# Loading q and k on 128 partitions instead of 96 in a fused attention and two-layer feed-forward kernel

## The chip, the cores and the metric

The kernel runs on one core of a Trainium2 chip. A core has a matmul engine (TensorE, in the profile PE, with PEld for its weight loads), a vector engine (DVE), a scalar engine (ACT), a general engine (POOL) and a queue engine (SP) that here issues nearly all transfers; sixteen DMA engines carry them. Each engine works through its own list of instructions in order and waits on semaphores for the others. The metric is device microseconds (us) of one execution, lower is better.

## The reference, cut to what matters

```python
def sm_attn(qq, kk, vv):                       # scale = 1/8
    s = scale * qq @ kk.T ; s = s - max(s) ; a = exp(s)
    return (a / (sum(a) + 1e-9)) @ vv
p_packed = sm_attn(p, k, v)                    # 32 packed rows read 576 tokens
out      = sm_attn(q, p_packed, p_packed)      # 576 tokens read the 32 rows
x = out as (4*576, 8*64)
g = softplus(x @ w_in) ; x = g @ w_out         # 512 -> 2048 -> 512
out = (sigmoid(x @ w_gate) * (x @ w_val)) @ w_out2   # 512 -> 1536 -> 512
```

q, k and v are (4 batches, 8 heads, 576 tokens, 64), in 32-bit floats; p has 32 rows in place of 576. The weights come in 64-bit floats and are made 32-bit on the chip.

## The kernel before, in words

Attention is cut into eight units u0 to u7: a batch and half of its heads (four). Each unit needs one load of k, q and v (576 KB each, four heads) and a small one of p. `load_kqv` (L216) issues the loads in the order of a plan as soon as the memory region given for it is free: k0, k1, q0, v0, q1, v1, then k2, q2, v2, k3 and so on. A load puts 96 partitions to use: partition r takes six neighbouring tokens (6r to 6r+5) of each of the four heads, so a contiguous piece is 6 x 64 numbers, 1536 bytes.

`attn_unit` (L367) is a generator of stages with a `yield` between them:

- k to its transposed form kT: `by_chunk` (L335) lets POOL copy one pair of heads from the loaded tile into x, [96, 6, 2, 64]; `tr_pair` (L344) then lets TensorE transpose six blocks of 96 tokens x 128 columns into two PSUM banks, from which ACT copies 288 columns each (L356). Twice, for two pairs of heads. kT's tokens then lie as c*96 + r for token 6r + c.
- s1 (L387): p against kT; the first softmax on DVE and ACT (L395 to L407, in place in a1, normalised at L407).
- q the same way as k into qT (L409 to L414).
- a1 transposed in six blocks of 96 tokens (L421), copied by ACT to a1T (L422).
- the product with v (L440), twelve filler matmuls for the first three units (L365), the result copied by ACT into bdT (L94).
- s2 (L465): q against the packed rows; the second softmax on DVE, ACT and POOL (L475 to L483), transposed (L493) and split in two parts as operand A2h, A2l of the feed-forward layers.

Since a1's tokens lie in the same order as v's (both six to a partition), L421 takes neighbouring columns. The token order of q goes through the whole feed-forward part, and the final store undoes it with a view of the output (L992, L1016).

Units 0 to 3 run ahead; then the first layer (L111 to L113 inside `emit_h`, after the first weights are folded with the packed rows at L570) starts, and units 4 to 7 are slipped between its matmuls. Beside that, weights are loaded into a ring of two raw tiles and converted on DVE by three instructions each (L178, L183, L187); each conversion done lets SP issue the next weight load (L153, L155). The tile framework orders each engine's list by its own planning, so a change of shapes can also change the order of instructions. A DMA that takes one of eight completion semaphores waits until the DMA eight places earlier on it has landed.

Of the kernel before, what the change touches and what calls it, by code (L numbers as in the profile page):

```python
# [9 lines left out]
F32 = mybir.dt.float32  # L10
F32R = mybir.dt.float32r
I32 = mybir.dt.int32
AF = mybir.ActivationFunctionType
ALU = mybir.AluOpType
# [6 lines left out]
def attn_moe_moe_kernel(  # L21
# [21 lines left out]
    nc = tc.nc  # L43
    B, H, S, D = q.shape
# [4 lines left out]
    P = 128  # L49
    NC = 6  # L50
    CT = S // NC
    HS = S // 2
    CF = 256
    NCH1 = F1 // CF
    NCH2 = F2 // CF
# [12 lines left out]
    VCH = 8  # L68
    VSP = 0
# [14 lines left out]
    xa = cst.tile([P, KD * NT], F32, name="xa")  # L84
# [4 lines left out]
    def bank1():  # L89
        return ps_o[-1].tile([P, 512], F32, tag="o", name="ps1")  # L90
# [26 lines left out]
    att = tc.alloc_tile_pool(name="att", bufs=1, side="right")  # L117
# [14 lines left out]
    for c in range(NCH1):  # L132
        order += [("in", c, f) for f in range(2)] + [("out", c, f) for f in range(2)]
        if c > ECS:
            n = -(-len(early) // (NCH1 - c))
# [78 lines left out]
    KQV = 4 * NC * D  # L214

    def load_kqv():  # L216
        while plan and plan[0][2] not in busy:
            nm, u, tag = plan.popleft()
            b, g = divmod(u, 2)
            if tag == 6:  # L220
                t = att.tile([CT, KQV], F32, tag="acc6", name=f"{nm}{u}")
            else:
                t = xa[:CT, KQV * tag : KQV * (tag + 1)]
            src = {"k": k, "q": q, "v": v}[nm][b, 4 * g : 4 * g + 4]
            if nm == "v" and u >= VCH:
                t = t.rearrange("p (c h d) -> p c h d", c=NC, h=4)
                for hh in range(4):
                    nc.sync.dma_start(t[:, :, hh], src[hh].rearrange("(r c) d -> r c d", c=NC)) if VSP else None
                if not VSP:
                    nc.sync.dma_start(t, src.rearrange("h (r c) d -> r c h d", c=NC))  # L230
            else:
                t = t.rearrange("p (h c d) -> p h c d", h=4, c=NC)
                nc.sync.dma_start(t, src.rearrange("h (r c) d -> r h c d", c=NC))
            if nm == "k" and u + 1 < 2 * B:
                load_p(u + 1)
            kqv[nm, u] = t
            busy[tag] = (nm, u)
# [24 lines left out]
    ident = cst.tile([P, P], F32, name="ident")  # L262
# [56 lines left out]
    MULA = 0  # L319
# [6 lines left out]
    E1 = nc.scalar  # L326
# [5 lines left out]
            :, :, :NK  # L332
        ]

    def by_chunk(src, j):  # L335

        x = att.tile([CT, NC, 2, D], F32, tag="x", bufs=2, name="x")
        nc.gpsimd.tensor_scalar(
            x, src[:, 2 * j : 2 * j + 2].rearrange("p h c d -> p c h d"), 1.0, 0.0,
            op0=ALU.mult, op1=ALU.add,  # L340
        )
        return x

    def tr_pair(src, j, dst, eng):  # L344
        x = by_chunk(src, j)
        for hf in range(2):
            ps = bank1()
            for c in range(3):
                nc.tensor.transpose(
                    ps[:, c * CT : (c + 1) * CT],  # L350
                    x[:, 3 * hf + c].rearrange("p h d -> p (h d)"),
                    ident[:CT, :CT],
                )
            o = dst[:, j, hf * HS : (hf + 1) * HS]
            if eng is nc.scalar:
                eng.activation(o, ps[:, :HS], AF.Copy)  # L356
            else:
                eng.tensor_copy(o, ps[:, :HS])

    def warm(u, to, n):  # L360

# [5 lines left out]
    def attn_unit(u):  # L367
        b, g = divmod(u, 2)
# [3 lines left out]
        for e in range(2):  # L372
            r = slice(64 * e, 64 * e + 64)
# [2 lines left out]
            )  # L376
        kt = kqv.pop(("k", u))
        kT = att.tile([P, 2, S], F32, tag="kT", bufs=1, name="kT")
        tr_pair(kt, 0, kT, nc.scalar)
        yield  # L380
        tr_pair(kt, 1, kT, E1)
        done_kqv("k", u)
        yield
        s1 = bank2()
# [16 lines left out]
        )  # L401
        nc.vector.tensor_scalar(mx[:, 2:3], mx[:, 2:3], 1e-9, None, op0=ALU.add)
        nc.vector.reciprocal(mx[:, 3:4], mx[:, 2:3])
        if MULA:
            nc.scalar.activation(a1, a1, AF.Copy, scale=mx[:, 3:4])
        else:
            nc.vector.tensor_scalar(a1, a1, mx[:, 3:4], None, op0=ALU.mult)  # L407
        yield
        qt = kqv.pop(("q", u))  # L409
        qT = att.tile([P, 2, S], F32, tag="qT", bufs=2, name="qT")  # L410
        tr_pair(qt, 0, qT, nc.scalar)
        yield
        tr_pair(qt, 1, qT, E1)
        done_kqv("q", u)  # L414
        yield
        a1T = att.tile([CT, NC, P], F32, tag="a1T", bufs=2, name="a1T")
        for hf in range(2):
            pa = bank1()
            for c in range(3):
                o = (3 * hf + c) * CT  # L420
                nc.tensor.transpose(pa[:CT, c * P : (c + 1) * P], a1[:, o : o + CT], ident)  # L421
            nc.scalar.activation(  # L422
                a1T[:, 3 * hf : 3 * hf + 3].rearrange("p c n -> p (c n)"),
                pa[:CT, : 3 * P], AF.Copy,
            )
# [563 lines left out]
        add(v1, u, v1)  # L989
        result(s1, v1, 0)  # L990

    outv = out.rearrange("(b r c) m -> b c r m", r=CT, c=NC)  # L992
    NTT = HB * S // P

    def emit_out2(ps, c, t):
# [15 lines left out]
        if c == NCH2 - 1:  # L1011
            t0 = ps * HB * S + t * P
            a, e = t0, t0 + P
            while a < e:
                b, r = divmod(a, S)
                cc, r = divmod(r, CT)  # L1016
                n = min(e - a, CT - r)
                eng = nc.scalar if ps and a > t0 else nc.sync
                eng.dma_start(outv[b, cc, r : r + n, :], acc[a - t0 : a - t0 + n])
                a += n  # L1020
# [65 lines left out]
```

## Time and profile before

| | us |
|---|---|
| median of three timed runs (866.4 to 867.51) | 866.66 |
| span of the profiled execution, first to last instruction | 864.4 |
| what lies around the span, taken as the difference | 2.3 |
| TensorE busy in the span | 840.7 |
| granted TensorE clock | 1.000 |

The profile has one execution; its own time is listed only as its span, so the difference of 2.3 us to the median stands for what lies around it. TensorE is busy for 97% of the span, which says that little time is left in waits, and where the rest of 24 us lies: in the first 60 us most of all, before and while the attention units run ahead. A busy TensorE isn't at its peak, since matmuls overlap in its pipeline and their ends are modelled.

### The profile page before, as it was taken

Reading aid. Unit: us, or ns where it says so; the run is one execution under the profiler, and the core shown is the slowest. Engines: PE = TensorE matmul, PEld = TensorE weight load, DVE = VectorE, ACT = ScalarE, POOL = GpSimd, SP = SyncE. Lnnn points to the kernel's source line nnn. Section 1 sums busy time; section 2 is a strip of 40 time slices with the busy share of each in tenths; the row PEclk is TensorE's granted clock in tenths of the full one; section 3 lists DMA queues with packets and bytes.
Section 4 is the critical chain, followed back from the end, with each engine's and each line's share of the span. In section 5 each row is a group of like instructions: output and inputs, shape, how many; then the busy total and the mean of one; then the engine's idle time right before and its main releaser. Section 6 shows DMA issues by size and latency. Waiting matters only on the chain. (4 is left out here: it accounts for less than half of the span.)

```text
span 864.4 us, 15635 instructions
## 1 busy us (share of the span) xinstructions
PE 840.7 (97%) x6100; PEld 789.8 (91%) x6100; DVE 618.2 (72%) x1051; ACT 401.1 (46%) x721; POOL 474.7 (55%) x453
## 2 busy tenths in 40 slices
PE   6899999999999999999899999999999999999997
PEld 5788999899999999999898999999988999999995
DVE  2875556957576767668898788887896756767665
ACT  4567565576666656677533432222352432322210
POOL 4454333235555545685569787876984734536400
PEclk9999999999999999999999999999999999999999
DMA  9984330303023412300055555644515313213003
GB/s 237 225 212 91 82 82 3 92 7 99 2 96 101 127 27 82 119 26 1 1 165 187 161 164 148 201 129 131 162 53 156 112 47 86 67 43 111 14 1 109
DMA packets 58009, 85.55 MB, mean 99 GB/s; under 512 B 6352, under 2 KB 39248, under 8 KB 57936
## 3 DMA queue, kind: packets, MB, share of 16 engines
q1 hardware_dynamic: 56928, 83.31, 34.3%
q10 hardware_dynamic: 1008, 1.25, 0.4%
q8 instruction: 48, 0.79, 0.4%
q14 instruction: 25, 0.20, 0.1%
HBM read 65.67 MB, written 18.87 MB: 98 GB/s over the span
## 5 line engine op out<-in xcount | busy, mean ns | idle before, releaser
L111 PE MATMUL bank<-aop,BH 128*128 128x288 f32 x672 | 199.2, 296 | 3.1 <-DVE work L954 1.4
L113 PE MATMUL bank<-aop,BL 128*128 128x288 f32 x672 | 198.8, 296 | 0.6 <-POOL BL L99 0.6
L112 PE MATMUL bank<-aop,BH 128*128 128x288 f32 x672 | 197.8, 294 | 0.2 <-DVE aop L99 0.2
L99 POOL TENSOR_TENSOR ghl<-g,ghl 128x576 fp32r<-128x576 f32 x64 | 93.7, 1465 | 133.0 <-ACT ghl L106 132.8
L653 PE MATMUL ps<-ghl,woh 128*128 128x288 f32 x512 | 148.7, 305 | 3.0 <-DVE xa L661 2.6
L661 DVE TENSOR_TENSOR xa<-xa,ps 128x288 f32<-128x288 f32 x224 | 98.4, 449 | 70.4 <-PE ps L656 70.1
L654 PE MATMUL ps<-ghl,wol 128*128 128x288 f32 x512 | 143.3, 295 | 0.0
L111 PEld LDWEIGHTS bank<-aop,BH 128*128 128x128 f32 x672 | 126.2, 188 | 9.3 <-issue 1.5
L112 PEld LDWEIGHTS bank<-aop,BH 128*128 128x128 f32 x672 | 126.4, 188 | 4.1 <-DVE aop L99 0.4
L113 PEld LDWEIGHTS bank<-aop,BL 128*128 128x128 f32 x672 | 126.5, 188 | 0.9 <-POOL BL L99 0.9
L99 POOL TENSOR_TENSOR BL<-cv,BH 128x512 fp32r<-128x512 f32 (+1 forms) x96 | 117.9, 1243 | 4.9 <-ACT BH L106 3.8
L656 PE MATMUL ps<-ghl,woh 128*128 128x288 f32 x512 | 109.0, 294 | 0.1
L653 PEld LDWEIGHTS ps<-ghl,woh 128*128 128x128 f32 x512 | 96.2, 188 | 6.0 <-issue 2.4
L654 PEld LDWEIGHTS ps<-ghl,wol 128*128 128x128 f32 x512 | 96.3, 188 | 0.5
L954 DVE TENSOR_TENSOR work<-work,bank 128x576 f32<-128x576 f32 (+1 forms) x100 | 70.8, 724 | 29.2 <-PE bank L113 29.0
L1002 PE MATMUL ps<-ol,gv 128*128 128x512 f32 x216 | 84.9, 393 | 0.0
L1001 PE MATMUL ps<-oh,gv 128*128 128x512 f32 x216 | 84.4, 391 | 0.5 <-ACT gv L967 0.4
L1003 PE MATMUL ps<-oh,gv 128*128 128x512 f32 x216 | 84.8, 393 | 0.0
L983 ACT ACTIVATE work<-bank 128x576 f32<-128x576 f32 (+1 forms) x25 | 15.8, 634 | 143.8 <-DVE bank L954 143.8
L656 PEld LDWEIGHTS ps<-ghl,woh 128*128 128x128 f32 x512 | 82.1, 188 | 0.3 <-POOL ghl L99 0.3
L1009 DVE TENSOR_TENSOR xa<-xa,ps 128x512 f32<-128x512 f32 x90 | 61.5, 684 | 28.3 <-PE ps L1003 27.8
L111 PE MATMUL ps<-A2h,wph 128*128 128x288 f32 x256 | 77.6, 303 | 0.1
(126 smaller groups left out, 1747.9 us busy)
## 6 DMA issues: line engine op xcount, KB each, us to landing
cv<-B SPq DMA_DIRECT2D x52, 256.0 KB, 2.7
B<-cv SPq DMA_DIRECT2D x48, 256.0 KB, 4.2
raw_in<-in_moe_w_in_dram SPq DMA_DIRECT2D x16, 512.0 KB, 3.7
raw_out<-in_moe_w_out_dram SPq DMA_DIRECT2D x16, 512.0 KB, 3.6
raw_g<-in_moe_w_gate_dram SPq DMA_DIRECT2D x12, 512.0 KB, 4.4
raw_v<-in_moe_w_val_dram SPq DMA_DIRECT2D x12, 512.0 KB, 4.6
raw_o<-in_moe_w_out_dram SPq DMA_DIRECT2D x12, 512.0 KB, 4.2
xa<-in_q_dram SPq DMA_DIRECT2D x6, 576.0 KB, 7.0
```

The source lines that it names most:

```text
L99: eng.tensor_tensor(lo, x, hi.bitcast(F32), op=ALU.subtract)
L111: nc.tensor.matmul(ps, wh, xh, start=first, stop=False)
L112: nc.tensor.matmul(ps, wh, xl, start=False, stop=False)
L113: nc.tensor.matmul(ps, wl, xh, start=False, stop=last)
L653: nc.tensor.matmul(out_, wh[:, ms], gh[:, f], start=f == 0, stop=False)
L654: nc.tensor.matmul(out_, wl[:, ms], gh[:, f], start=False, stop=False)
L656: nc.tensor.matmul(out_, wo_hl[c, f][0][:, ms], gl[:, f], start=False, stop=f == 1)
L661: nc.vector.tensor_tensor(dst, dst, out_, op=ALU.add)
L954: nc.vector.tensor_tensor(to, x, y, op=ALU.add)
L1001: nc.tensor.matmul(bank, gh[:, ts_], oh, start=f == 0, stop=False)
L1002: nc.tensor.matmul(bank, gh[:, ts_], ol, start=False, stop=False)
L1003: nc.tensor.matmul(bank, gl[:, ts_], oh, start=False, stop=f == 1)
```

## The change

q and k are loaded on all 128 partitions: for each pair e of two heads, 64 partitions with nine neighbouring tokens each (a contiguous piece of 9 x 64 numbers, 2304 bytes). That takes two DMAs per load in place of one, e = 0 into partitions 0 to 63 and e = 1 into 64 to 127. v stays as it was, on 96 partitions. `turn` replaces `by_chunk` and `tr_pair`: three times per load POOL copies three token places of both pairs, [128, 3, 2, 64], TensorE transposes three blocks of 128 x 128 into one bank, and ACT copies 384 columns. The tokens of k, and so of a1, now lie as c*64 + r for token 9r + c, those of v still six to a partition; the normalisation of the first softmax therefore writes a new tile a1n in token order (a step of nine numbers), and the transposes of a1n read it with a step of six numbers. The output view follows q's order.

```diff
+    NQ = 9
+    RQ = S // NQ
...
-            if nm == "v" and u >= VCH:
...
-            else:
-                t = t.rearrange("p (h c d) -> p h c d", h=4, c=NC)
-                nc.sync.dma_start(t, src.rearrange("h (r c) d -> r h c d", c=NC))
+            else:
+                t = t[:, : 2 * NQ * D].rearrange("p (i x) -> p i x", i=2)
+                for e in range(2):
+                    nc.sync.dma_start(
+                        t[RQ * e : RQ * e + RQ],
+                        src[2 * e : 2 * e + 2].rearrange("i (r c) d -> r i (c d)", c=NQ),
+                    )
+                t = t.rearrange("p i (c d) -> p c i d", c=NQ)
...
+    def turn(src, n, dst):
+        x = att.tile([P, 3, 2, D], F32, tag="x", bufs=3, name="x")
+        nc.gpsimd.tensor_scalar(x, src[:, 3 * n : 3 * n + 3], 1.0, 0.0, op0=ALU.mult, op1=ALU.add)
+        ps = bank1()[:, : 3 * P]
+        for c in range(3):
+            nc.tensor.transpose(
+                ps[:, c * P : (c + 1) * P], x[:, c].rearrange("p i d -> p (i d)"), ident
+            )
+        nc.scalar.activation(
+            dst[:, :, 3 * RQ * n : 3 * RQ * (n + 1)].rearrange("p e (c r) -> p e c r", r=RQ),
+            ps.rearrange("p (c e r) -> p e c r", e=2, r=RQ), AF.Copy,
+        )
...
-        tr_pair(kt, 0, kT, nc.scalar)
-        yield
-        tr_pair(kt, 1, kT, E1)
+        for n in range(3):
+            turn(kt, n, kT)
+            if n == 1:
+                yield
...
-            nc.vector.tensor_scalar(a1, a1, mx[:, 3:4], None, op0=ALU.mult)
+        a1n = att.tile([P, S], F32, tag="a1n", bufs=1, name="a1n")
+        nc.vector.tensor_scalar(
+            a1n.rearrange("p (r c) -> p c r", c=NQ), a1.rearrange("p (c r) -> p c r", c=NQ),
+            mx[:, 3:4], None, op0=ALU.mult,
+        )
...
-                nc.tensor.transpose(pa[:CT, c * P : (c + 1) * P], a1[:, o : o + CT], ident)
+                nc.tensor.transpose(
+                    pa[:CT, c * P : (c + 1) * P],
+                    a1n.rearrange("p (r c) -> p c r", c=NC)[:, 3 * hf + c], ident,
+                )
...
-    outv = out.rearrange("(b r c) m -> b c r m", r=CT, c=NC)
+    outv = out.rearrange("(b r c) m -> b c r m", r=RQ, c=NQ)
```

The change moves instructions too. On ACT, around the copies of unit 1's packed rows into bdT (line L94 before, L96 after), with the exponentials of unit 0's second softmax (L479), the list before reads:

```order
L94 ACTIVATE bdT<-ps_279 64x2x32 x2
L422 ACTIVATE a1T<-ps_319 96x384
L422 ACTIVATE a1T<-ps_324 96x384
L479 ACTIVATE a_337<-a_337 96x384
L94 ACTIVATE bdT<-ps_361 64x2x32
L479 ACTIVATE a_353<-a_353 96x384
L94 ACTIVATE bdT<-ps_361 64x2x32
```

and after:

```order
L96 ACTIVATE bdT<-ps_275 64x2x32 x2
L422 ACTIVATE a1T<-ps_316 96x384
L422 ACTIVATE a1T<-ps_321 96x384
L479 ACTIVATE a_334<-a_334 96x384
L479 ACTIVATE a_350<-a_350 96x384
L96 ACTIVATE bdT<-ps_358 64x2x32 x2
```

The second exponential has moved from between the two copies of unit 1 to ahead of both.

On DVE, where the first two w_in tiles are converted (L178, L183, L187 before; L180, L185, L189 after) beside unit 1's first softmax (mx, a_225 or a1n) and unit 0's second (m, a), the list before reads:

```order
L178 TENSOR_SCALAR w_in<-raw_in 128x4x128
L402 TENSOR_SCALAR mx<-mx 128x1
L183 SCALAR_TENSOR_TENSOR w_in<-raw_in,w_in 128x4x128
L403 RECIPROCAL mx<-mx 128x1
L187 SCALAR_TENSOR_TENSOR w_in<-raw_in,w_in 128x4x128
L407 TENSOR_SCALAR a_225<-a_225,mx 128x576
L178 TENSOR_SCALAR w_in<-raw_in 128x4x128
L183 SCALAR_TENSOR_TENSOR w_in<-raw_in,w_in 128x4x128
L187 SCALAR_TENSOR_TENSOR w_in<-raw_in,w_in 128x4x128
L475 TENSOR_REDUCE m_336<-ps_329 96x12
L476 TENSOR_TENSOR a_337<-ps_329,m_336 96x384
```

and after:

```order
L401 TENSOR_SCALAR a1n<-a_227,mx 128x9x64
L180 TENSOR_SCALAR w_in<-raw_in 128x4x128
L185 SCALAR_TENSOR_TENSOR w_in<-raw_in,w_in 128x4x128
L189 SCALAR_TENSOR_TENSOR w_in<-raw_in,w_in 128x4x128
L180 TENSOR_SCALAR w_in<-raw_in 128x4x128
L185 SCALAR_TENSOR_TENSOR w_in<-raw_in,w_in 128x4x128
L475 TENSOR_REDUCE m_333<-ps_326 96x12
L475 TENSOR_REDUCE m_349<-ps_342 96x12
L476 TENSOR_TENSOR a_334<-ps_326,m_333 96x384
L476 TENSOR_TENSOR a_350<-ps_342,m_349 96x384
L189 SCALAR_TENSOR_TENSOR w_in<-raw_in,w_in 128x4x128
```

Unit 1's first softmax now stands ahead of the conversions, and the last conversion of the second tile behind four instructions of unit 0's second softmax.

On SP, from the third k load on (raw_out is a load of w_out, k_305 and k_301 are k3), before:

```order
L233 DMA xa<-in_k_dram 96x4x384
L153 DMA raw_out<-in_moe_w_out_dram 128x1024
L282 DMA p<-in_p_dram 128x64
L153 DMA raw_out<-in_moe_w_out_dram 128x1024
L282 DMA p<-in_p_dram 128x64
L233 DMA xa<-in_q_dram 96x4x384
L233 DMA xa<-in_v_dram 96x4x384
L233 DMA k_305<-in_k_dram 96x4x384
```

and after:

```order
L233 DMA xa<-in_k_dram 64x2x576 x2
L155 DMA raw_out<-in_moe_w_out_dram 128x1024
L286 DMA p<-in_p_dram 128x64 x2
L155 DMA raw_out<-in_moe_w_out_dram 128x1024
L233 DMA xa<-in_q_dram 64x2x576 x2
L229 DMA xa<-in_v_dram 96x4x384
L233 DMA k_301<-in_k_dram 64x2x576 x2
```

The loads keep their order; each load of q and k has become two rows, and q2, v2 and k3 still stand behind the second w_out load.

## Rows read from the trace of the kernel before

**Rows 1.** The page: busy time of the engines, and TensorE in forty slices of 21.6 us.

```profile
PE 840.7 (97%) x6100; PEld 789.8 (91%) x6100; DVE 618.2 (72%) x1051; ACT 401.1 (46%) x721; POOL 474.7 (55%) x453
PE   6899999999999999999899999999999999999997
```

**Rows 2.** Windows: stretch, length, busy time of PE, PEld, DVE, ACT, POOL, clock, DMA share, GB/s.

```profile
3.00:18.00 15.00, 10.84 (x63) 9.02 (x64) 2.66 (x7) 6.10 (x20) 6.84 (x9) 1.00 1.11 252
18.00:21.00 3.00, 2.61 (x59) 2.38 (x57) 1.28 (x5) 2.43 (x8) 0.00 (x0) 1.00 1.11 343
21.00:40.00 19.00, 16.71 (x181) 14.00 (x178) 15.09 (x39) 8.85 (x26) 8.06 (x10) 1.00 0.99 236
40.00:60.00 20.00, 18.64 (x194) 16.03 (x193) 16.43 (x33) 13.97 (x35) 10.29 (x9) 1.00 0.83 200
60.00:160.00 100.00, 99.33 (x962) 91.55 (x963) 62.31 (x148) 61.47 (x138) 38.14 (x38) 1.00 0.28 67
```

**Rows 3.** Timeline of POOL: start, duration, instruction, count, idle time before and releaser.

```profile
5.97 1.63 POOL L338 TENSOR_SCALAR x<-xa 96x768 f32<-96x768 f32 x2 [2.67 <-DMA xa<-in_k_dram]
11.72 0.83 POOL L338 TENSOR_SCALAR x<-xa 96x768 f32<-96x768 f32 x1 [1.04 <-DMA xa<-in_q_dram]
...
16.27 1.63 POOL L338 TENSOR_SCALAR x<-xa 96x768 f32<-96x768 f32 x2 [1.78 <-PE ps L387]
```

**Rows 4.** Timeline of TensorE from 16 to 40 us.

```profile
16.08 0.66 PE L349 MATMUL ps<-ident,x 96*128 96x96 f32 x6
17.15 0.71 PE L349 MATMUL ps<-ident,x 96*128 96x96 f32 x6 [0.41 <-POOL x L338]
17.70 0.82 PE L421 MATMUL ps<-ident,a 128*96 128x128 f32 x6
...
19.89 1.24 PE L440 MATMUL ps<-a1T,xa 96*64 96x32 f32 x36 [0.39 <-ACT a1T L422]
...
23.26 2.25 PE L465 MATMUL ps<-bdT,qT 128*96 128x64 f32 x24
...
29.53 2.25 PE L465 MATMUL ps<-bdT,qT 128*96 128x64 f32 x24 [0.96 <-ACT bdT L94]
...
36.84 0.47 PE L493 MATMUL ps<-ident,a 96*128 96x96 f32 x3 [0.66 <-POOL a L483]
37.63 0.47 PE L493 MATMUL ps<-ident,a 96*128 96x96 f32 x3 [0.32 <-POOL a L483]
...
39.81 0.40 PE L111 MATMUL ps<-A2h,wph 128*128 128x288 f32 x1
```

**Rows 5.** Timeline of ACT around 29 us.

```profile
28.61 0.22 ACT L94 ACTIVATE bdT<-ps 64x64 f32<-64x64 f32 x1 [2.38 <-PE ps L365]
28.73 0.51 ACT L479 ACTIVATE a<-a 96x384 f32<-96x384 f32 x1
29.26 0.22 ACT L94 ACTIVATE bdT<-ps 64x64 f32<-64x64 f32 x1
```

**Rows 6.** Groups by line and shape, first 300 us: count, busy us, mean ns, idle before.

```profile
L349 PE MATMUL ps<-ident,x 96*128 96x96 f32 x192 | 23.6, 262 | 0.9 <-POOL x L338 0.4 <-ACT pT L374 0.3
...
L356 ACT ACTIVATE kT<-ps 128x288 f32<-128x288 f32 x32 | 11.9, 410 | 4.4 <-PE ps L387 3.2 <-PE ps L349 0.6
...
L422 ACT ACTIVATE a1T<-ps 96x384 f32<-96x384 f32 x16 | 7.0, 484 | 0.6 <-PE ps L421 0.6
...
L421 PE MATMUL ps<-ident,a 128*96 128x128 f32 x48 | 6.8, 274 | 0.0
...
L407 DVE TENSOR_SCALAR a<-a,mx 128x576 f32<-128x576 f32 x8 | 4.3, 537 | 0.2
```

**Rows 7.** Timeline of TensorE's weight loads at 25 us.

```profile
25.44 1.48 PEld L440 LDWEIGHTS ps<-a1T,xa 96*64 96x64 f32 x48
```

**Rows 8.** Timeline of SP: issues of the second w_out load and of q2.

```profile
23.84 0.33 SPq L153 DMA_DIRECT2D raw_out<-in_moe_w_out_dram  x1
...
24.74 0.38 SPq L233 DMA_DIRECT2D xa<-in_q_dram  x1
```

More of the change, by code (lines that the diff above doesn't have):

```diff
@@ L220, in load_kqv @@
             if tag == 6:
-                t = att.tile([CT, KQV], F32, tag="acc6", name=f"{nm}{u}")
+                t = att.tile([P, KQV], F32, tag="acc6", name=f"{nm}{u}")
             else:
-                t = xa[:CT, KQV * tag : KQV * (tag + 1)]
+                t = xa[:, KQV * tag : KQV * (tag + 1)]
             src = {"k": k, "q": q, "v": v}[nm][b, 4 * g : 4 * g + 4]
-            if nm == "v" and u >= VCH:
[L226 to L230, printed above, removed]
-            else:
-                t = t.rearrange("p (h c d) -> p h c d", h=4, c=NC)
-                nc.sync.dma_start(t, src.rearrange("h (r c) d -> r h c d", c=NC))
+            if nm == "v":
+                t = t[:CT].rearrange("p (h c d) -> p h c d", h=4, c=NC)
+                nc.sync.dma_start(t, src.rearrange("h (r c) d -> r h c d", c=NC))
+            else:
+                t = t[:, : 2 * NQ * D].rearrange("p (i x) -> p i x", i=2)
[5 more added lines that the diff above has]
+                t = t.rearrange("p i (c d) -> p c i d", c=NQ)
             if nm == "k" and u + 1 < 2 * B:
@@ L333, in heads @@
         ]
-    def by_chunk(src, j):
-        x = att.tile([CT, NC, 2, D], F32, tag="x", bufs=2, name="x")
+    def turn(src, n, dst):
+        x = att.tile([P, 3, 2, D], F32, tag="x", bufs=3, name="x")
         nc.gpsimd.tensor_scalar(
-            x, src[:, 2 * j : 2 * j + 2].rearrange("p h c d -> p c h d"), 1.0, 0.0,
-            op0=ALU.mult, op1=ALU.add,
-        )
[L342 to L356, printed above, removed]
-            else:
-                eng.tensor_copy(o, ps[:, :HS])
+            x, src[:, 3 * n : 3 * n + 3], 1.0, 0.0, op0=ALU.mult, op1=ALU.add
+        )
+        ps = bank1()[:, : 3 * P]
[7 more added lines that the diff above has]
+        )
     def warm(u, to, n):
@@ L403, in attn_unit @@
         nc.vector.reciprocal(mx[:, 3:4], mx[:, 2:3])
-        if MULA:
-            nc.scalar.activation(a1, a1, AF.Copy, scale=mx[:, 3:4])
-        else:
-            nc.vector.tensor_scalar(a1, a1, mx[:, 3:4], None, op0=ALU.mult)
+        a1n = att.tile([P, S], F32, tag="a1n", bufs=1, name="a1n")
[3 more added lines that the diff above has]
+        )
         yield
@@ L410, in attn_unit @@
         qT = att.tile([P, 2, S], F32, tag="qT", bufs=2, name="qT")
-        tr_pair(qt, 0, qT, nc.scalar)
-        yield
-        tr_pair(qt, 1, qT, E1)
+        for n in range(3):
+            turn(qt, n, qT)
+            if n == 1:
+                yield
         done_kqv("q", u)
@@ L419, in attn_unit @@
             for c in range(3):
-                o = (3 * hf + c) * CT
-                nc.tensor.transpose(pa[:CT, c * P : (c + 1) * P], a1[:, o : o + CT], ident)
+                nc.tensor.transpose(
+                    pa[:CT, c * P : (c + 1) * P],
+                    a1n.rearrange("p (r c) -> p c r", c=NC)[:, 3 * hf + c], ident,
+                )
             nc.scalar.activation(
@@ L1015, in emit_out2 @@
                 b, r = divmod(a, S)
-                cc, r = divmod(r, CT)
-                n = min(e - a, CT - r)
+                cc, r = divmod(r, RQ)
+                n = min(e - a, RQ - r)
                 eng = nc.scalar if ps and a > t0 else nc.sync
```

## The prediction

> **What bounds the kernel now.** I read the page first. TensorE is busy for 840.7 of 864.4 us, and in forty slices only the first two stand clearly under 9 [rows 1]. The reader is to see that 24 us of waits are all there is to win, and that the attention units that run ahead hold a good part of them. Next the windows [rows 2]: from 60 to 160 us, where units 4 to 7 lie between matmuls, TensorE is busy for 99.33 of 100 us, so an edit there pays only if it takes time from TensorE itself. From 3 to 18 us it is busy for 10.84 of 15, with the DMA engines full (share 1.11) at 252 GB/s; from 18 to 21 they are as full and move 343. Then who waits for what in this stretch: POOL's first copies of k0, q0 and q1 start at 5.97, 11.72 and 16.27, each after an idle time [rows 3]. The first two are put down to the transfer. The third is put down to a matmul, but q1 is fifth in the queue, and five loads of 589,824 bytes at 252 GB/s are 11.7 us, with the small loads of p and the start some 13 us after 3.0: I read 16.27 as q1's landing. TensorE goes on with it at 17.15 after 0.41 us of waiting [rows 4]. So up to q1 the transfers set the pace; behind it a chain through unit 1's scores (29.53), the second softmax (37.63) and the first layer (39.81) does.
>
> **The loads.** 128 partitions are reached by two DMAs of 64 each, issued one behind the other. No row shows a DMA of 64 rows. The stretch at 252 GB/s is mostly loads of 96 rows, that at 343 is w_in's, of 128 rows [rows 2]; 343 x 96/128 is 257, so the rate goes with the rows that a single DMA reaches, even though the 96-row loads lie back to back in the queue. From below, two DMAs of 64 rows that don't overlap would run at 343 x 64/128 = 172 GB/s, 3.43 us a load; from above, full overlap gives 343 and 1.72 us; now it is 2.34. As the 96-row loads show next to no overlap, I go a sixth of the way from 172 to 343: 200 GB/s, 2.95 us, 0.61 more. Four such loads land up to q1 (k0, k1, q0, q1): 4 x 0.61 = **+2.44 us**.
>
> The Trainium skill ("SBUF — State Buffer", section "Can I just issue two DMAs to hit both halves?") says that two DMAs on the two halves of the partitions run nearly one after the other, 6% better than one, since the ports are chosen for each transfer by itself; its section "Door 1: The DMA port swizzle" gives 196 GB/s for 64 partitions and 1 MiB. The estimate from that is 208 GB/s, 2.84 us a load, +2.0 in place of +2.44 and 867.4 in all; no row here shows 64 partitions, and the trace's proportion of 252 to 343 points the same way.
>
> **After q1 has landed.** Before, POOL needs 0.83 us for the first piece [rows 3]; a piece is now half as long per partition (384 for 768), about 0.42, so the first transposes start 0.41 earlier. At most more is won: a1T's second copy let the last three quarters of L440 start at 19.89, 3.62 after the landing [rows 3, 4]. Now the second piece is ready at 0.84, six transposes and six of a1n follow (to about 1.9), and the second copy of 0.48 [rows 6] ends near 2.5: 1.07 earlier. Between 0.41 and 1.07 I take the middle, **-0.74**.
>
> **Unit 1's packed rows.** The copy into bdT waits for the filler matmuls, then unit 0's exponential of 0.51 us runs between its two halves, and L465 waits 0.96 [rows 4, 5]. In the changed list both exponentials stand ahead of both copies: **-0.51**, if they are done by then. Unit 0's scores end about 25.5 (23.26 + 2.25), and the copies came at 28.6; both move with q1, so 3 us are left for four DVE instructions and two exponentials of 0.51. At worst nothing is won.
>
> **What costs nothing.** The waits at 36.84 and 37.63 (0.66 and 0.32) stay: POOL's products wait for the softmax that L465 starts, 8.1 us from 29.53 to 37.63, and no link of it gets shorter. TensorE's own work: with the pipeline's tail taken off, a 96-column transpose takes (0.66 - 0.262)/5 = 0.080 us and one of 128 takes (0.82 - 0.274)/5 = 0.109 [rows 4, 6]; a unit has 24 x 0.080 = 1.91 before and 18 x 0.109 = 1.97 after. Eight units: +0.4 at most, taken as 0. ACT gives back per unit 8 x 0.410 - 6 x 0.484 = 0.38, POOL some 0.8; neither is waited for behind 60 us, so 0. The new normalisation writes with a step of nine numbers; even at twice its 0.537 [rows 6] it would be done while TensorE waits for q1, and later it lies beside other work. a1n's weight loads read with a step of 24 bytes. L440's 64-column loads follow each other every 1.48/48 = 0.031 us [rows 7], so 96 neighbouring columns need about 0.046, hidden in 0.109 until the step makes them 2.4 times as slow; at four times it is 48 x (0.185 - 0.109) = +3.6. I take 0 and keep the end. SP's sixteen more issues lie in its idle time; the output goes in as many pieces as before.
>
> The Trainium skill (same page, section "Door 1: The DMA port swizzle", its note on cachelines) says that each access that crosses into another 16-byte line pays a penalty; by that a step of 24 bytes is slow, without a figure, and nothing here shows it for weight loads.
>
> **The sum.** +2.44 - 0.74 - 0.51 = +1.2 us. The profiled execution's span of 864.4 becomes 865.6; with the 2.3 us by which the median of 866.66 lies above the span, 867.9. A shift at 40 us stays to the end, since TensorE is nearly full from there on [rows 2].
>
> **The rivals.**
> - *No overlap at all (slower).* At 172 GB/s a load is 1.09 us longer: 4 x 1.09 = 4.36, less 0.74 and 0.51: +3.1, 869.8; if the exponentials come late, 870.3. For it: 252 is so near to 257. Against: the queue can start the upper half on engines that are done with the lower. It decides from about 183 GB/s downwards, where the sum passes 0.2% of the time, 1.73 us.
> - *The halves overlap (faster).* At 252 the loads cost nothing and the sum is -1.25: 865.4. At 343 q1 would land 2.5 us earlier, but TensorE can't use all: 0.6 at its start, the idle 0.39 from 18 to 21 us, and 0.5 from 3 to 18 (4.16 less 3.7 before the first matmul, which POOL's first piece lets start near 6.7) [rows 2, 3], so -1.5 - 0.51 = -2.0: 864.7. For it: the queue holds both DMAs at once. Against: the proportion above.
> - *q2, v2 and k3 late behind a conversion (slower).* They are issued behind the second w_out load, which waits for the last conversion of w_in's second tile. That conversion now stands behind unit 0's second softmax on DVE, after 25.5 plus the shift; the issue of q2, at 24.74 [rows 8], moves beyond 28. w_out 1.5, q2 2.95, v2 2.34 and k3 2.95 make 9.7 us of transfers, and k3 lands at 40 to 42. It is needed behind the first layer's matmuls, which started at 39.81 [rows 4], so about 42.5 with the shift. From there each us costs one: at +2 on the forecast, 869.9. Against: by these numbers k3 is there 0.5 to 2.5 us in time.
> - *The change moves nothing that counts.* The chain behind q1 has waits of 2.3 us between 21 and 40 [rows 2] and could take the shift up: 866.7.
>
> **How the numbers follow.** What this kernel's timing tells from no change is about 0.2%, 1.73 us. The forecast (rates of 183 to 225 GB/s) has 0.45 and by itself reaches from 866.8 to 868.9; no overlap 0.2; overlap 0.2; the late queue 0.1; the shift absorbed 0.05. Faster by over 1.73 us is the lower part of overlap and orders of other engines that I have not worked out: 0.18. Slower: no overlap, most of the late queue, the upper end of the forecast and a1n's slow reads: 0.38. The rest, 0.44, is within. The range takes 343 GB/s at one end and no overlap with nothing won at the other: 864.7 to 870.3.
>
> **What would show it.** The rate from 3 to 18 us: about 215 GB/s (v's two of six loads stay as they are) bears the forecast out, under 200 the first rival, 252 or more the second. POOL's first copy of q1 should start at 18.7, about 0.42 long, and TensorE should wait some 2 us just before. L465 of unit 1 should start 0.5 us after the filler matmuls, not 0.96. A wait for k3 after the first L111 matmuls speaks for the third rival. The forecast is wrong if TensorE's first layer starts before 39.8, or after 43.

## The result and the profile after

The changed kernel takes 875.14 us (median of 4 runs, 874.25 to 877.24), beside 867.09 for the kernel before on the same chip: a ratio of 1.0092, 95% interval 1.0074 to 1.0110. That is 8 us slower. I had forecast 867.9, within 864.7 to 870.3, so the time lies outside the range. The profiled execution has a span of 872.0 us in place of 864.4.

The windows of the changed kernel, in the stretches of [rows 2] (the same columns):

```profile
3.00:18.00 15.00, 10.71 (x40) 8.32 (x41) 1.23 (x5) 4.62 (x14) 5.28 (x12) 1.00 1.06 228
18.00:21.00 3.00, 2.38 (x19) 1.97 (x17) 2.01 (x4) 1.72 (x5) 0.94 (x2) 1.00 1.11 295
21.00:40.00 19.00, 16.03 (x204) 14.25 (x204) 14.26 (x36) 8.10 (x23) 4.92 (x7) 1.00 0.71 174
40.00:60.00 20.00, 15.41 (x132) 13.35 (x133) 12.83 (x23) 12.16 (x26) 9.79 (x13) 0.83 0.80 168
60.00:160.00 100.00, 97.28 (x951) 90.09 (x950) 67.57 (x148) 61.76 (x133) 38.70 (x47) 1.00 0.36 90
```

The loads at the start run at 228 GB/s, between the 252 of before and my 215. But most is lost later: from 40 to 60 us TensorE works 3.2 us less than before, and its granted clock is 0.83 on average (1.00 is 2.4 GHz, the lower level is 1.2). TensorE's timeline (start, duration, instruction, count, idle time before and what ended it) shows where:

```profile
11.46 4.05 PE L383 MATMUL ps<-kT,pT 128*128 128x288 f32 x8
...
16.60 2.14 PE L383 MATMUL ps<-kT,pT 128*128 128x288 f32 x8
18.58 1.15 PE L347 MATMUL ps<-ident,x 128*128 128x128 f32 x9
...
21.47 0.52 PE L347 MATMUL ps<-ident,x 128*128 128x128 f32 x3 [1.09 <-ACT qT L350]
...
31.72 2.25 PE L465 MATMUL ps<-bdT,qT 128*96 128x64 f32 x24 [0.54 <-ACT bdT L96]
...
42.28 0.40 PE L113 MATMUL ps<-A2h,wph 128*128 128x288 f32 x1
...
48.90 2.93 PE L347 MATMUL ps<-ident,x 128*128 128x128 f32 x12 [4.30 <-POOL x L342]
...
54.71 0.51 PE L113 MATMUL ps<-A2h,wph 128*128 128x288 f32 x1
```

The first layer starts at 42.28, 2.47 us behind the 39.81 of [rows 4]. Then TensorE waits 4.30 us for a turned copy on GpSimd (POOL), and after that wait twelve transposes take 2.93 us, where nine took 1.15 at 18.58. The second step of the first layer, at 54.71, began at 45.89 before:

```profile
45.89 0.49 PE L111 MATMUL ps<-A2h,wph 128*128 128x288 f32 x1
```

That is 8.8 us, of which 7.6 are left at the end of the span. GpSimd's timeline:

```profile
17.44 0.99 POOL L342 TENSOR_SCALAR x<-xa 128x384 f32<-128x384 f32 x2 [0.86 <-DMA xa<-in_q_dram]
...
44.04 1.77 POOL L101 TENSOR_TENSOR wol<-cv,woh 128x512 fp32r<-128x512 f32 x1 [2.62 <-ACT woh L108]
47.09 1.27 POOL L101 TENSOR_TENSOR wol<-cv,woh 128x512 fp32r<-128x512 f32 x1 [1.29 <-ACT woh L108]
48.33 0.99 POOL L342 TENSOR_SCALAR x<-k 128x384 f32<-128x384 f32 x2
```

The copy that TensorE waits for is k3's (x<-k, 48.33), and it has no wait of its own: GpSimd was at work on wol, the remainders of the two converted w_out tiles, and waited for them. k3's data had been there for 3.2 us by then: the second of its two transfers was issued at 33.88 and took 11.2 us from issue to landing, which makes 45.1 (SP's row, then that of the DMA view). TensorE's wait had begun at 44.6, so 0.5 us of it belong to the transfer and most of the rest to GpSimd's list.

```profile
33.88 0.72 SPq L233 DMA_DIRECT2D k<-in_k_dram  x1
```

```profile
k<-in_k_dram SPq DMA_DIRECT2D x1, 288.0 KB, 11.2
```

The remainders come from ScalarE (woh), and woh from the conversions on VectorE, whose timeline (the ScalarE rows below it in a fence of their own) reads:

```profile
18.00 1.27 DVE L401 TENSOR_SCALAR a1n<-a,mx 128x576 f32<-128x576 f32 x1
19.10 0.73 DVE L391 TENSOR_REDUCE mx<-ps 128x1 f32<-128x576 f32 x1
...
29.56 0.68 DVE L189 SCALAR_TENSOR_TENSOR w_in<-raw_in,w_in 128x512 int32<-128x512 int32 x1
...
42.86 1.31 DVE L401 TENSOR_SCALAR a1n<-a,mx 128x576 f32<-128x576 f32 x1
44.00 0.69 DVE L185 SCALAR_TENSOR_TENSOR cv<-raw_out,cv 128x512 int32<-128x512 int32 x1
44.73 1.63 DVE L189 SCALAR_TENSOR_TENSOR cv<-raw_out,cv 128x512 int32<-128x512 int32 x1
```

```profile
20.11 0.74 ACT L394 ACTIVATE a<-ps,mx 128x576 f32<-128x576 f32 x1 [0.52 <-DVE mx L392]
...
46.39 0.63 ACT L108 ACTIVATE woh<-cv 128x512 fp32r<-128x512 f32 x1 [1.11 <-DVE cv L189]
```

So the chain is: normalisation of unit 2 (42.86), last two parts of w_out's conversion (44.00, 44.73), woh (46.39), wol (47.09), k3's copy (48.33), k3's transposes (48.90). One link is longer than elsewhere: the last part of the conversion took 1.63 us, where the same operation on a w_in tile, at 29.56, took 0.68, and it overlaps GpSimd's first remainder, which took 1.77 where the second took 1.27. Two links are new. First the order on GpSimd. Before, in order:

```
L483 TENSOR_TENSOR a_418<-a_418,m_417 96x384
L338 TENSOR_SCALAR x<-k_305 96x768
L338 TENSOR_SCALAR x<-xa 96x768
L338 TENSOR_SCALAR x<-k_305 96x768
L99 TENSOR_TENSOR wol<-cv,woh 128x512
```

and after:

```
L483 TENSOR_TENSOR a_415<-a_415,m_414 96x384
L342 TENSOR_SCALAR x<-xa 128x384 x2
L101 TENSOR_TENSOR wol<-cv,woh 128x512 x2
L342 TENSOR_SCALAR x<-k_301 128x384 x2
```

k3's copies stood ahead of the second remainder, with the first long done; now they stand behind both. Nothing in the diff touches these lines. Second the normalisation, which was priced at 0:

```profile
L401 DVE TENSOR_SCALAR a1n<-a,mx 128x576 f32<-128x576 f32 x8 | 10.4, 1296 | 0.3
```

1296 ns in place of 537 [rows 6]. It stands in the chain above, and at the start as well: TensorE ends unit 1's scores near 18.7 (16.60 and 2.14), but their maximum starts at 19.10, behind unit 0's normalisation (18.00); its exponential (20.11) and behind that q1's copies on ScalarE come later, and q1's last transposes wait 1.09 us. Once, in a later unit, TensorE waits for a1n itself (the second row is from a_split_plain, a kernel below in which the normalisation is in order again; its L415 is L418):

```profile
126.28 0.89 PE L418 MATMUL ps<-ident,a1n 128*96 128x128 f32 x6 [0.84 <-DVE a1n L401]
```

```profile
120.77 0.89 PE L415 MATMUL ps<-ident,a 128*96 128x128 f32 x6 [0.16 <-DVE a L401]
```

There was another suspect. SP issued q2 at 30.65, not 24.74 [rows 8], behind the second w_out load:

```profile
30.27 0.33 SPq L155 DMA_DIRECT2D raw_out<-in_moe_w_out_dram  x1
30.65 1.91 SPq L233 DMA_DIRECT2D xa<-in_q_dram  x2
...
33.24 1.36 SPq L233 DMA_DIRECT2D k<-in_k_dram  x2
```

That is the held queue of my third rival, and I took it for the cause at first; the experiments say otherwise.

### The profile page after: what moved, and what is told of

The parts are those of the page before. It is cut to its first block, busy times and chain, and to the rows that moved or that the text cites. A ratio compares the mean times of both kernels' runs of the same rounds, so it can differ in the third digit from the quotient of the medians.

```text
span 872.0 us, 15604 instructions
## 1 busy us (share of the span) xinstructions
PE 842.3 (97%) x6052; PEld 791.5 (91%) x6052; DVE 626.0 (72%) x1051; ACT 400.9 (46%) x705; POOL 473.0 (54%) x469
## 4 chain that ended last, share of the span: by engine, by line
PE 84%; DVE 7%; POOL 4%; ACT 2%; issue 2%; DMA 1%; SPq 0%; POOLq 0%; ACTq 0%; DVEq 0%
PE bank L115 9%; PE bank L113 9%; PE bank L114 9%; PE ps L653 7%; PE ps L654 7%; PE ps L656 7%; PE ps L1003 5%; PE ps L1002 5%; PE ps L1001 5%; PE ps L113 4%; PE ps L115 4%; PE ps L114 4%; PE ps L590 2%; PE ps L465 2%; PE ps L383 2%
## 5 line engine op out<-in xcount | busy, mean ns | idle before, releaser
L113 PE MATMUL bank<-aop,BH 128*128 128x288 f32 x672 | 199.1, 296 | 2.0 <-DVE work L954 0.8
L113 PEld LDWEIGHTS bank<-aop,BH 128*128 128x128 f32 x672 | 126.2, 188 | 8.0 <-ACT work L971 0.8
L113 PE MATMUL ps<-A2h,wph 128*128 128x288 f32 x256 | 77.5, 303 | 0.0
```

Of the source, the lines that this page charges most:

```text
L113: nc.tensor.matmul(ps, wh, xh, start=first, stop=False)
```

## The experiments

Ratios are to the kernel before, run on the same chip, with 95% intervals.

**First round: is it the held queue, or the normalisation?** Four kernels, each one edit. (Kernel a_... starts from the changed kernel, b_... from the one before.)

```diff
# a_xr, b_xr: the first w_out load goes to a free part of xa
-    XR = 0
+    XR = 1
# a_read: write in order, read with a step
-            a1n.rearrange("p (r c) -> p c r", c=NQ), a1.rearrange("p (c r) -> p c r", c=NQ),
+            a1n.rearrange("p (r c) -> p r c", c=NQ), a1.rearrange("p (c r) -> p r c", c=NQ),
# a_actn: the normalisation on ScalarE
-        nc.vector.tensor_scalar(
+        nc.scalar.activation(
```

> The changed kernel with XR = 1: the first of the two w_out loads lands in a free part of xa, so the second needs no buffer that the conversion of w_in's second tile must free; q2, v2 and k3 no longer stand behind that conversion on SP. Theory 1 (the held queue): the four idle microseconds of the DMA engines at 28 to 32 us go, k3 lands 3 to 5 us earlier (43 to 45 us instead of 48.3), TensorE's wait of 4.30 us at k3's first transposes shrinks below 1.5, and the time falls by 4 to 7 us, from 875.1 to 868 to 871. Theory 2 (the 64-row transfers are slow by themselves) and theory 3 (the new normalisation's 1.27 us on VectorE): the transfers and the normalisation are as they were, so at most 1.5 us go: 873.6 to 875.1.

> The kernel before with the same XR = 1, as the control. Theory 1: there the conversion of w_in's second tile had ended at 23.81 us and the transfers stood back to back, so nothing is freed: within 1 us of 867.1. If XR = 1 by itself is worth several microseconds (860 to 864), a gain of the changed kernel by it says nothing of the held queue.

> The changed kernel with the reordering normalisation writing in order and reading its source with a step of 64 elements, in place of reading in order and writing with a step of 9. Order of the instructions unchanged. If the strided write is what makes it cost 1.27 us on VectorE, it falls to between 0.52 and 0.7 us. Theory 3 (this instruction's 0.74 us more, eight times, is the loss): the time falls by 4 to 6 us to 869 to 871. Theory 1: the conversion that holds the queue still stands behind unit 0's second softmax, which waits for TensorE, so the queue opens at most 1.5 us earlier: 873 to 875.

> The changed kernel with the reordering normalisation on ScalarE in place of VectorE. VectorE is relieved of 8 x 1.27 us, ScalarE takes 8 x 0.8 to 1.5 us. Theory 3: 869 to 872. Theory 1: as long as the last conversion of w_in's second tile stands behind unit 0's second softmax, 873 to 876.

Measured: a_xr 874.33 (1.0085 [1.0070, 1.0101]), b_xr 869.76 (1.0029 [1.0018, 1.0040]), a_read 874.13 (1.0078 [1.0061, 1.0095]), a_actn 876.04 (1.0099 [1.0083, 1.0115]). The queue was free in a_xr (DMA share 0.97 from 21 to 40 us) and next to nothing was won: theory 1 missed. But a_xr also moved instructions on every engine. b_xr, the same edit to the kernel before, lost 2.7 us: there too every engine's list moved, and the early w_out load, issued at 10.50, shares the queue, with q1's copy at 17.62 in place of 16.27. So neither tells of the held queue alone, and a cleaner test was due. (The expectations of a_xr and a_free1 take 48.3 for k3's landing; that is where its copy starts, and it landed at 45.1.) The normalisation takes 776 ns with a strided read (a_read, in which every engine's list is the changed kernel's) and 1374 on ScalarE (a_actn, in which other instructions moved too). So most of its added time was the strided write's, but with 520 of its 1296 ns gone a_read gave back 1.0 us, no more than the intervals leave open.

**Second round: the same with the order held.** a_free1 puts the second w_out load into xa and gives its issue a lower priority, so that TensorE's and ScalarE's orders stay those of the changed kernel.

```diff
# a_free1 (a_free1_read: with a_read's edit as well)
-        if XR and key == ("out", 0, 0):
+        if XR and key == ("out", 0, 1):        # XR = 1
...
+            with tc.high_priority(-100) if key == ("out", 0, 1) else nullcontext():
# a_plainnorm
+        a1n = a1
+        nc.vector.tensor_scalar(a1, a1, mx[:, 3:4], None, op0=ALU.mult)
# b_reorder, cut: the normalisation of before writes a1n for six tokens a partition,
# and the transposes read a1n with that step
...
+                a1n.rearrange("p (r c) -> p c r", c=NC), a1.rearrange("p (c r) -> p c r", c=NC),
```

> The changed kernel with one wait taken away and the order of all engines left as it is but for two neighbours: the second w_out load lands in a free part of xa and is issued behind q2, so q2, v2 and k3 wait for no conversion of w_in on VectorE; TensorE's and ScalarE's instructions stand in the same order as in the changed kernel, and k2's turning still stands ahead of the second softmax's products on GpSimd. Theory 1 (the held queue): q2 is issued at about 25 us in place of 30.65, k3 lands at 42 to 44 us in place of 48.3, TensorE's wait of 4.30 us and the 0.83 clock of 40 to 60 us go, and the time falls by 4 to 7 us to 868 to 871. Theory 4 (the wait moves on: the units' own chain over VectorE and GpSimd ends as late without the held queue): 873 to 875, with TensorE waiting for GpSimd's products or VectorE instead of k3.

> As a_free1, and the reordering normalisation writes in order and reads with a step (0.78 us instead of 1.29 us measured on VectorE). Theory 1 with the normalisation's time as the smaller part: 0.3 to 1.5 us below a_free1, 867 to 870. Theory 4: as a_read, 873 to 875.

> The changed kernel with the normalisation in place and in order, without the reordering to v's tokens (this part of the computation is left out, so the output isn't the reference's). It takes 0.52 us again, and VectorE's order puts the last conversion of w_in's second tile ahead of unit 0's second softmax, as in the kernel before. Theory 1: the queue opens at 24 to 25 us, the time falls to 867 to 870. Theory 2 (the 64-row transfers as such): 872 to 875, since they are unchanged.

> The kernel before with one part of the change alone: its normalisation writes a second tile through a strided pattern (128 x 6 x 96, step of 6 elements) and the transposes read it with that step; loads as before, output the reference's. On VectorE the second unit's normalisation now stands ahead of two of w_in's conversions, and the last conversion of w_in's second tile still stands ahead of unit 0's second softmax. Theory 1: the queue isn't held behind the second softmax, so at most 1 to 2 us more: 867 to 869. Theory 3 (the instruction's own 0.75 us, eight times): 871 to 873.

a_free1 took 874.59 (1.0083 [1.0065, 1.0102]) and a_free1_read 875.35 (1.0082 [1.0058, 1.0106]). In a_free1 SP issued q2 more than 4 us earlier, and k3's copy still came at 48.71, behind wol (SP, then GpSimd):

```profile
26.40 1.25 SPq L234 DMA_DIRECT2D xa<-in_q_dram  x2
```

```profile
47.48 1.27 POOL L101 TENSOR_TENSOR wol<-cv,woh 128x512 fp32r<-128x512 f32 x1 [1.29 <-ACT woh L108]
48.71 0.99 POOL L343 TENSOR_SCALAR x<-k 128x384 f32<-128x384 f32 x2
```

Theory 1 falls with this, and GpSimd's queue becomes theory 5. a_plainnorm, which leaves out the reordering to v's tokens, took 872.03 (1.0055 [1.0035, 1.0075]); its GpSimd order is the changed kernel's, and VectorE gets to the conversions sooner. More than the instruction's length differs in it: w_in's last conversion stands ahead of unit 0's second softmax, so that q2 is issued at 26.87, and ScalarE copies q1 ahead of unit 1's exponential. b_reorder, 867.03 (1.0002 [0.9991, 1.0013]), says that the reordering by itself costs the kernel before nothing; but its write, with a step of six, takes 799 ns there, not 1296.

**Third round: k3 out from behind wol.** The two remainders go to VectorE, and TensorE's order and the queue's stay those of the changed kernel.

```diff
# a_split; a_free1_split and a_free1_split_read with the edits above; b_split from before
-        split_lo(nc.gpsimd, lo, x, hi)
+        split_lo(nc.vector if key in [("out", 0, 0), ("out", 0, 1)] else nc.gpsimd, lo, x, hi)
# b_two, cut: before, with two transfers per load of q and k, 96 rows and 2 heads each
...
+                    for e in range(2):
+                        nc.sync.dma_start(t[:, 2 * e : 2 * e + 2], v_[:, 2 * e : 2 * e + 2])
```

> The changed kernel with the two first remainders of w_out (wol, the subtraction behind the two conversions of w_out's first chunk) on VectorE in place of GpSimd; TensorE's order and the queue's are the changed kernel's. Theory 1 (the queue held by w_in's conversion makes k3 late) alone: nothing changes, 874 to 876. Theory 5 (on GpSimd k3's turning stands behind these two remainders, which wait for w_out's conversions on VectorE and ScalarE until 47.09 us): k3's turning starts when k3 is there, by the 10.6 us from issue to landing at about 44 us in place of 48.33, TensorE's wait of 4.30 us shrinks below 1.5, and the time falls by 2 to 6 us to 869 to 873.

> Both at once: q2, v2 and k3 not held by w_in's conversion (a_free1) and the two remainders of w_out on VectorE (a_split). Theory 5 with both causes needed: k3 is there at about 40 us and its turning starts by 42 us, TensorE doesn't wait for it and its clock stays at 1.00 from 40 to 60 us; 867 to 871, at least 2 us below a_free1. If the time is lost elsewhere: 873 to 876 again.

> As a_free1_split with the normalisation that writes in order and reads with a step (0.78 us in place of 1.29). Theory 5: 0 to 1 us below a_free1_split, 866.5 to 870; the least that the changed layout can come to if what is left is the loads at the start.

> The kernel before with one part of the change alone: each load of q and k in two transfers, of 96 rows and 2 heads each. Theory 2a (the number of transfers costs): q1's turning, at 16.27 us in the kernel before and at 17.44 in the changed one, starts at 17 us or later, and the time rises by 1 us or more. Theory 2b (the 64 rows cost): q1 as before within 0.3 us, and the time within 1 us of 867.

a_split took 871.25 (1.0058 [1.0041, 1.0074]), a_free1_split 870.86 (1.0056 [1.0041, 1.0071]), a_free1_split_read 869.49 (1.0041 [1.0026, 1.0056]). With the split, k3's copy starts when its data are there (GpSimd, then TensorE, of a_split):

```profile
41.53 1.11 POOL L342 TENSOR_SCALAR x<-k 128x384 f32<-128x384 f32 x2 [0.57 <-DMA k<-in_k_dram]
```

```profile
45.28 0.55 PE L347 MATMUL ps<-ident,x 128*128 128x128 f32 x3 [0.17 <-POOL x L342]
...
47.43 0.97 PE L418 MATMUL ps<-ident,a1n 128*96 128x128 f32 x6 [1.60 <-ACT kT L350]
```

The 4.30 us are down to 0.17, and a new wait of 1.60 for ScalarE's copies follows. k3 had landed by 41.53, with the queue held as in the changed kernel (its loads issued from 32.49). The queue, held or free, makes no difference that can be told with the split or without. The control came in the next round: b_split 867.03 (1.0000 [0.9990, 1.0010]). So the split by itself is worth nothing where k3 doesn't stand behind it, as far as one control shows in which other instructions moved too.

b_two missed both expectations: 871.01 (1.0050 [1.0028, 1.0072]), though q1's copies, at 15.91 and 16.98, were not late. So two transfers in place of one don't delay q1, but they moved the lists of all engines from 37 us on. TensorE was 1.9 us late at the first layer's second step (47.77 for 45.89) and lost more at 55 us, in waits for ScalarE and at half speed behind them (24 matmuls in 3.89 us, 2.25 in [rows 4]):

```profile
55.24 3.89 PE L470 MATMUL ps<-bdT,qT 128*96 128x64 f32 x24 [1.95 <-ACT bdT L94]
```

**Fourth round: TensorE's cold start.** Unit 0's scores (L383) take 4.05 us in the changed kernel; nine idle matmuls ahead were to bring its speed up earlier.

```diff
# a_warm, a_all_warm (from a_free1_split_read), b_warm
+    for _ in range(9):
+        nc.tensor.matmul(pw[:, :P], ident, ident, start=True, stop=True)
```

> The changed kernel with nine matmuls of the identity by itself on TensorE before the first transpose, while nothing else is there to do; all other instructions in the changed kernel's order. Theory 6 (TensorE's first matmuls take 506 ns in place of 266 because it has not worked before, and in the changed kernel this lasts until unit 0's scores are through): unit 0's scores, at 11.46 to 15.5 us now, take 2.1 us instead of 4.05, the wait of 1.09 us for qT's copies shrinks, L570 comes at 38.3 to 39.7 us instead of 40.49, and the time falls by 1 to 2.5 us: 872.5 to 874. Theory 2 (the transfers' rate alone sets the start): under 0.5 us.

> a_free1_split_read with the nine matmuls ahead; order otherwise that of a_free1_split_read. Theory 6: 1 to 2.5 us below its 869.5, that is 867 to 868.5, about level with the kernel before. Theory 2: 869 to 870.

> The kernel before with the same nine matmuls ahead, as control. Here the first matmuls are slow until 11.8 us only, and q1's data bind soon after, so less is to be had: 0 to 1.5 us below 867, 865 to 867. The added matmuls move instructions on VectorE and TensorE from 20 us on, which the runs so far show to be worth up to 3 us either way.

> The kernel before with w_out's first two remainders on VectorE, as control for a_split. There k3's turning stands ahead of the second remainder on GpSimd already and only the first (31.16 us) is ahead of it, long done. Theory 5: no gain, 866 to 869. If the split helps by itself: 862 to 864.

a_warm 874.37 (1.0082 [1.0067, 1.0097]), a_all_warm 870.42 (1.0032 [1.0018, 1.0046]), b_warm 870.97 (1.0045 [1.0027, 1.0063]): nothing won anywhere, and b_warm, whose order moved, lost. In a_warm TensorE waited 1.47 us for k1's copy and was slow again:

```profile
10.37 1.54 PE L350 MATMUL ps<-ident,x 128*128 128x128 f32 x6 [1.47 <-POOL x L345]
11.70 4.05 PE L386 MATMUL ps<-kT,pT 128*128 128x288 f32 x8
```

In a_all_warm the scores took 2.86 us and L574 (L570 in the changed kernel's numbers) came at 39.17, 1.8 us earlier than without; but behind the wait of 1.78 us at 38.77 the first layer's matmuls took 0.44 us each in place of 0.29, until 43.4, and what was gained was gone:

```profile
38.77 0.47 PE L497 MATMUL ps<-ident,a 96*128 96x96 f32 x3 [1.78 <-POOL a L487]
39.17 1.11 PE L574 MATMUL ps<-w_in,bdT 128*64 128x256 f32 x8
...
42.00 0.44 PE L114 MATMUL ps<-A2l,wph 128*128 128x288 f32 x1
```

Theory 6 is left without support as a loss of its own; a_warm, in which the scores were as slow as without, is no test of it.

**Last round: what the loads cost.**

```diff
# a_split_plain: a_split with a_plainnorm's edit.  a_128:
-                for e in range(2):
-                    nc.sync.dma_start(
-                        t[RQ * e : RQ * e + RQ],
-                        src[2 * e : 2 * e + 2].rearrange("i (r c) d -> r i (c d)", c=NQ),
-                    )
+                nc.sync.dma_start(
+                    t, src.rearrange("h (r i c) d -> (h r) i (c d)", i=2, c=NQ)
+                )
```

> a_split with the normalisation in place and in order (the reordering to v's tokens is left out, so the output isn't the reference's). If the two causes found add up (a_split 3.9 us below the changed kernel, the plain normalisation 3 us below it): 867.5 to 869, and what is left is the 1.2 us worked out for the loads before the result. If they are one loss counted twice: 870 to 872.

> The changed kernel with each load of q and k as one transfer of 128 rows of 4,608 bytes (tokens land in other places, so the output isn't the reference's); instructions from 25 us on stand in another order. If 64 rows a transfer is what the rate suffers from: 250 GB/s or more between 3 and 18 us in place of 228, q1's turning at 16.3 us or earlier in place of 17.44, and L570 at 39.3 us or earlier in place of 40.49. If not: 225 to 240 GB/s, q1 at 17 to 17.6. Of the whole time either says little, since the order differs: 866 to 875.

a_split_plain took 868.84 (1.0018 [1.0006, 1.0031]): both edits take 6.5 us away, each by itself 3.0, so the two causes add up within the noise, and 1.6 us are left. a_128 loads at 250 GB/s and has q1's copy at 16.27, where it was before. As b_two, with as many transfers, had 251 GB/s, and the shorter pieces of before ran at 252, the 64 rows of a transfer are what slows the loads. L570 came at 44.09, not by 39.3 as expected; a_128's 872.22 (1.0058 [1.0039, 1.0076]) is another order's, with a wait of 4.01 us for a1T (window, GpSimd, TensorE of a_128):

```profile
3.00:18.00 15.00, 11.17 (x54) 9.38 (x55) 2.49 (x5) 6.02 (x17) 6.22 (x13) 1.00 1.04 250
```

```profile
16.27 1.46 POOL L340 TENSOR_SCALAR x<-xa 128x384 f32<-128x384 f32 x3 [3.18 <-DMA xa<-in_q_dram]
```

```profile
23.38 2.13 PE L438 MATMUL ps<-a1T,xa 96*64 96x32 f32 x36 [4.01 <-ACT a1T L420]
```

Together: of the 8.0 us, wol ahead of k3 makes 3.0 (a_split less the changed kernel, each against before: 5.1 for 8.05) to 3.5 (a_split_plain less a_plainnorm: 1.6 for 5.1), the normalisation and what it moves on VectorE and ScalarE 3.0 to 3.5 likewise, the loads and turnings 1.6. By the intervals each of the first two is uncertain by about 2 us. How the normalisation's part divides between its length and the moved instructions isn't shown: where 520 ns of the length went and every list stayed, the time fell by 1.0 us (a_read) and 1.4 (a_free1_split_read against a_free1_split), and rose by 0.8 in a_free1_read. None of these kernels is faster than the kernel before.

## Why the prediction was wrong, by its own steps

**Up to the first layer the forecast stayed within its own bounds.** I had called it wrong if the first layer starts before 39.8 or after 43. It started at 42.28, 1.3 behind the 41.0 of the sum (39.81 and 1.2), and most of the loss came behind that.

**The loads (+2.44): right in kind, too large.** a_split_plain, in which the other causes are gone, shows the term (GpSimd, then TensorE; its L437, L462 and L567 are L440, L465 and L570 of before):

```profile
17.98 1.47 POOL L342 TENSOR_SCALAR x<-xa 128x384 f32<-128x384 f32 x3 [3.58 <-DMA xa<-in_q_dram]
```

```profile
18.55 1.03 PE L347 MATMUL ps<-ident,x 128*128 128x128 f32 x6 [1.59 <-POOL x L342]
...
21.63 1.24 PE L437 MATMUL ps<-a1T,xa 96*64 96x32 f32 x36 [0.55 <-ACT a1T L419]
...
30.85 2.25 PE L462 MATMUL ps<-bdT,qT 128*96 128x64 f32 x24 [0.54 <-ACT bdT L96]
...
39.42 1.08 PE L567 MATMUL ps<-w_in,bdT 128*64 128x256 f32 x8
...
49.93 0.51 PE L113 MATMUL ps<-A2h,wph 128*128 128x288 f32 x1
```

q1's copy starts 1.71 us behind [rows 3], not 2.44; in the changed kernel it is 1.17, in a_read 0.80 (17.07), so the term isn't known better than that. The wait of some 2 us just before it, 1.59 here, wasn't there in the changed kernel, where unit 0's slow scores (11.46) kept TensorE busy till then. The proportion from which the 200 GB/s came isn't borne out: in a_128 each load of q and k reaches 128 rows, and the stretch runs at 250, no faster than with 96. The Trainium skill's rule ("SBUF — State Buffer", section "Can I just issue two DMAs to hit both halves?"), by which I had estimated +2.0, was nearer; that two transfers of 64 rows don't reach what one of 128 does (228 and 250 GB/s) bears out its direction. A slip in the first rival: the sum passes 1.73 us at 191 GB/s, not at 183.

**After q1 has landed (-0.74): wrong.** 21.63 is 3.65 us behind 17.98; before it was 3.62 [rows 3, 4]. The smaller pieces brought nothing, since the second copy of a1T is waited for as before.

**Unit 1's packed rows (-0.51): right.** L465's wait is 0.54 for 0.96 [rows 4], 0.42 less.

1.71 + 0.03 - 0.42 makes the +1.32 at which L462 stands (30.85 for 29.53 [rows 4]), and 868.84 is 1.6 above its kernel before: the forecast's +1.2 came out nearly right there, with two errors that cancel. That the end agrees too is partly luck: in the same trace the first layer's second step, at 49.93, is 4.04 behind the 45.89 of before, and where the kernel makes that up I haven't followed.

**"What costs nothing": the step that failed.** I wrote of the normalisation that "even at twice its 0.537 it would be done while TensorE waits for q1, and later it lies beside other work". It took 2.4 times as long, and it didn't lie beside other work only: on VectorE unit 1's maximum stands behind it, and w_out's conversions do, and TensorE waits 0.84 us for it at 126.28. I had looked at who waits for a1n at the start, not at what is queued behind it. With it and the moves that its reordering brings, 3.0 to 3.5 us were costed at 0. The weight loads with a step of 24 bytes, for which I had kept +3.6, took 183 ns in place of 126 (means of 48) and cost nothing to be seen: six transposes of a1n at full speed take 0.82 us in a_free1, as many as in [rows 4].

**The third rival: right symptom, in the main another cause.** The wait for k3 behind the first L113 matmuls came, and I had named it as that rival's sign. k3 did land late, at 45.1 and not at 40 to 42, 0.5 us into TensorE's wait. But then its copy stood 3.2 us longer on GpSimd, behind two instructions that waited for VectorE. I had followed the moved instructions on SP, DVE and ACT and not on POOL, where two rows that now stand ahead of k3 cost 3.0 to 3.5 us. That the queue was held, as I had worked out, is true, and costs nothing that can be measured: in a_free1 k3's second half was issued at 29.45 and landed 11.1 us later, near 40.6, and the time was the same.

What set GpSimd's order so, the later k3 load, the third turning or something else in the change, stays open. The reverse test, k3 behind wol in the kernel before, was not tried.

## What to carry to other kernels

When an instruction grows, price it by what is queued behind it on its engine, not by who reads its result; an off-path engine's order is part of the change, so compare all engines' orders, and ask of each instruction that moved ahead of another what it waits for. A wait that ends in one engine's row ("<-POOL x") is followed one step further: where that row shows no wait of its own, look at the instruction ahead of it. And where controls that were to change next to nothing move the time by 2.7 us and more, as b_xr and b_two did, one edit's total says little below that; the trace at the place does.

## What the runs showed of the hardware

The same VectorE multiplication of 128 x 576 float32 numbers took 537 ns in order [rows 6], 799 ns writing with a step of 24 bytes (b_reorder), 1296 ns with a step of 36 bytes, and 776 ns when it wrote in order and read with a step of 256 bytes (a_read; each the mean of eight):

```profile
L401 DVE TENSOR_SCALAR a1n<-a,mx 128x576 f32<-128x576 f32 x8 | 6.2, 776 | 0.3
```

```profile
L408 DVE TENSOR_SCALAR a1n<-a,mx 128x576 f32<-128x576 f32 x8 | 6.4, 799 | 0.2
```

The matmuls' speed at the start isn't in the column of the granted clock: it reads 1.00 from 3 to 18 us in the changed kernel, while L383's eight took 4.05 us at 11.46 and 2.14 at 16.60. These eight took 3.53 us in a_split and 2.11 in a_split_plain, though nothing that is edited there comes before them, so such a stretch differs from profile to profile by itself. After the idle times of 4.30 us (changed kernel), 1.78 (a_all_warm) and 1.95 us (b_two) TensorE ran at about half speed for a while, and the granted clock of those stretches fell below 1.00; after 0.66 and 0.32 us [rows 4] it did not. The length of the wait alone doesn't decide: in a_free1_split_read the same 1.78 us, before 40.55, were followed by matmuls at full speed.

A conversion on VectorE (128 x 512, two inputs) took 1.63 us while GpSimd ran a subtraction of the same size, and 0.68 us at 29.56; GpSimd's took 1.77 beside it and 1.27 at 47.09.
